# Left-over tokens of an expert in half blocks of 64 on 64-column tiles of TensorE

## The chip, the cores and the metric

One core of one Trainium2 chip. Times are device microseconds (us) of one execution. The kernel is timed in several executions and its median is given; each profile is one execution, and its "span" is some 2 us shorter than the time taken for the same run. Everything is float32.

## The reference, cut to what matters

Sliding-window attention over 8 x 576 = 4608 tokens of width 512 is followed by a mixture of eight experts, in which each token takes one expert (its own best, or that of the token before it).

```python
B, S, D, E, F = (8, 576, 512, 8, 1024)
...
            if s == 0 or local_gate[b, s] < 0.5:
                e = fresh_e
            else:
                e = prev_e if prev_e >= 0 else fresh_e
...
            h = np.maximum(x[b, s] @ w1[e], 0.0)
            out[b, s] = p[e] * (h @ w2[e])
```

## The kernel before

The expert part works in blocks of tokens that share an expert. Six early blocks of 128 tokens come from the first three sequences; then eight big blocks of 256; what is left of each expert is rounded up to small blocks of 128. Eighteen small blocks run always, which is just enough for these inputs; up to three more stand under a condition. Each block fetches its expert's weights (two loads of 2 MB by SyncE) and gathers its rows (an indirect DMA, issued by GpSimd). TensorE then does, in order: first layer of block i, transposes of block i+1, second layer of block i. The output goes out as an indirect scatter, also issued by GpSimd.

```python
    def hidden(self, st, quiet, step):               # first layer
        n = len(st["slots"]) * P                     # 128 or 256 tokens
        each = 512 // n
        for g in range(FK // each):                  # FK = 8 pieces of the 1024 hidden columns
            hp = self.ps_h.tile([P, each, n], F32, name="hp")
            for i in range(each):
                m = g * each + i
                for kk in range(DK):                 # DK = 4
                    nc.tensor.matmul(hp[:, i, :], lhsT=st["w1"][:, kk, m * P:(m + 1) * P], rhs=st["xt"][:, kk, :n],
                                     start=(kk == 0), stop=(kk == DK - 1))
            ...                                      # ReLU on ScalarE or VectorE
    def result(self, st, step):                      # second layer
        for i, s in enumerate(st["slots"]):
            yp = self.ps_y.tile([P, D], F32, name="yp")
            for m in range(FK):
                nc.tensor.matmul(yp, lhsT=st["h"][:, m, i * P:(i + 1) * P], rhs=st["w2"][:, m, :],
                                 start=(m == 0), stop=(m == FK - 1))
            ...
            nc.scalar.activation(y, yp, Act.Copy, scale=st["pw"][:, s:s + 1])
            nc.gpsimd.indirect_dma_start(out=self.out[:, :], out_offset=..., in_=y, ...)
    def run(self, ctx, rt):
        ...
        used = nc.values_load(self.tabs["ej"][0:1, NBLK:NBLK + 1], ...)
        with tc.If(used > SURE):                     # extra blocks, asleep with these inputs
            for n in order[total:]:
                ...
```

After this part a check of the attention's range ("flag") decides on a second condition, the careful path, which is asleep too.

## Time and profile before

| | before |
|---|---|
| median of the first 3 runs | 737.21 us (736.51 to 738.21) |
| profiled run: time, span | 733.09 us, 731.3 us |
| attention, to the first expert matmul | 144.3 us |
| experts, to the start of TensorE's last second-layer matmul | 578.3 us |
| tail, from there to the end of the span | 8.7 us |

The three parts are cut at starts of TensorE instructions in the timeline.

### The profile page before, as it was taken

What the parts mean: (1) busy time and instruction counts of PE and PEld (TensorE: products, weight loads), DVE (VectorE), ACT (ScalarE), POOL (GpSimd) and SP (SyncE); (2) the same over time, 40 slices, a digit from 0 to 9 for tenths busy, and PEclk for the clock granted to TensorE, in tenths of its full rate; (3) what the DMA queues carried; (4) which work ended last, traced back from release to release, by engine and by line L of the source; (5) the groups of instructions that cost most, each with busy time, mean ns of one, the idle gap of its engine ahead of it and who ended that gap; (6) DMA issues with size and microseconds to landing.
All of it is one profiled execution on the core that took longest, in us unless ns stands there. A gap on an engine that the chain in (4) does not pass through costs nothing. (4 is left out here: it accounts for less than half of the span.)

```text
span 731.3 us, 12607 instructions
## 1 busy us (share of the span) xinstructions
PE 689.0 (94%) x5476; PEld 500.9 (68%) x5476; DVE 186.4 (25%) x433; ACT 130.6 (18%) x186; POOL 115.4 (16%) x128
## 2 busy tenths in 40 slices
PE   4879788799999999999999999999999999999995
PEld 3667676677767765766756757677767776776673
DVE  5866898739400101101101011000100010001000
ACT  2755455311111010110110100011001100110010
POOL 4311323111131111111111020111111111100010
PEclk9999999999999999999999999999999999999999
DMA  8999999998899854564465455688989889888500
GB/s 310 389 399 391 390 364 393 408 343 314 290 368 428 345 200 158 172 232 172 141 226 195 143 196 219 215 315 316 332 321 318 327 315 346 288 319 306 201 17 30
DMA packets 37555, 203.84 MB, mean 279 GB/s; under 512 B 3661, under 2 KB 3677, under 8 KB 29296
## 3 DMA queue, kind: packets, MB, share of 16 engines
q1 hardware_dynamic: 28544, 173.45, 65.0%
q0 software_dynamic: 8944, 29.45, 10.2%
q8 instruction: 47, 0.77, 0.4%
q14 instruction: 20, 0.16, 0.1%
HBM read 184.01 MB, written 19.92 MB: 279 GB/s over the span
## 5 line engine op out<-in xcount | busy, mean ns | idle before, releaser
L928 PEld LDWEIGHTS hp<-xt,w 128*128 128x128 f32 x2048 | 272.6, 191 | 28.7 <-issue 14.3
L928 PE MATMUL hp<-xt,w 128*128 128x128 f32 (+1 forms) x2048 | 287.7, 301 | 1.4 <-ACT xt L916 1.4
L942 PE MATMUL yp<-w,h 128*128 128x512 f32 x640 | 280.4, 592 | 0.0
L942 PEld LDWEIGHTS yp<-w,h 128*128 128x128 f32 x640 | 118.9, 190 | 136.8 <-issue 134.9
L932 DVE TENSOR_SCALAR h<-hp 128x512 f32<-128x512 f32 x34 | 23.5, 691 | 473.5 <-issue 362.0
L947 ACT ACTIVATE y<-yp,pw 128x512 f32<-128x512 f32 x40 | 27.5, 687 | 358.5 <-PE yp L942 336.2
L948 POOL DMA_INDIRECT out_dram<-y,idx x40 | 41.1, 1027 | 302.7 <-ACT y L947 275.9
L886 POOL DMA_INDIRECT xg<-xs,idx x40 | 40.2, 1004 | 208.1 <-PE tp L915 190.0
L253 PE MATMUL sp<-w 64*64 64x128 f32 (+1 forms) x1296 | 47.4, 281 | 12.8 <-DMA w<-in_q_dram 7.0
L253 PEld LDWEIGHTS sp<-w 64*64 64x64 f32 x1296 | 40.7, 144 | 24.6 <-issue 10.5
L934 ACT ACTIVATE h<-hp 128x512 f32<-128x512 f32 x46 | 27.5, 597 | 159.2 <-PE hp L928 159.2
L282 PE MATMUL xo<-vb,p 128*64 128x74 f32 x576 | 46.2, 231 | 8.0 <-issue 3.8
L272 DVE TENSOR_TENSOR p<-p,mask 128x1024 f32<-128x1024 f32 x36 | 47.0, 1305 | 21.4 <-ACT p L269 21.0
L282 PEld LDWEIGHTS xo<-vb,p 128*64 128x64 f32 x576 | 40.2, 137 | 13.1 <-issue 6.0
L282 PE MATMUL xo<-va,p 128*64 128x74 f32 x576 | 46.0, 231 | 2.7 <-issue 2.1
L269 ACT ACTIVATE p<-sp 128x1024 f32<-128x1024 f32 x36 | 36.9, 1024 | 49.7 <-PE sp L253 45.1
L282 PEld LDWEIGHTS xo<-va,p 128*64 128x64 f32 x576 | 40.1, 137 | 2.4 <-issue 1.6
L291 DVE TENSOR_TENSOR x<-xo,allr 128x512 f32<-128x512 f32 x36 | 24.5, 680 | 2.5 <-DMA xs<-x 2.5
L229 POOL COPY vb<-va 64x1184 f32<-64x1184 f32 x9 | 10.9, 1216 | 87.5 <-PE xo L282 56.3
L915 PE MATMUL tp<-ident,xg 128*128 128x128 f32 x160 | 22.8, 273 | 0.0
L916 DVE COPY xt<-tp 128x512 f32<-128x512 f32 x32 | 21.2, 679 | 0.0
L915 PEld LDWEIGHTS tp<-ident,xg 128*128 128x128 f32 x160 | 18.7, 142 | 0.9
(203 smaller groups left out, 199.3 us busy)
## 6 DMA issues: line engine op xcount, KB each, us to landing
w<-in_w_dram SPq DMA_DIRECT2D x64, 2048.0 KB, 8.8
va<-in_v_dram SPq DMA_DIRECT2D x9, 1184.0 KB, 12.5
vtt<-in_vt_dram SPq DMA_DIRECT2D x9, 1024.0 KB, 10.2
xs<-x POOLq DMA_DIRECT2D x9, 1024.0 KB, 12.6
w<-in_k_dram SPq DMA_DIRECT2D x17, 512.0 KB, 11.6
w<-in_q_dram SPq DMA_DIRECT2D x17, 512.0 KB, 13.4
xg<-xs,idx POOLq DMA_INDIRECT x40, 8.2
out_dram<-y,idx POOLq DMA_INDIRECT x40, 8.2
```

The costliest lines, as they stand in the source:

```text
L253: nc.tensor.matmul(sp[c * WIN:(c + 1) * WIN, j, a:b], lhsT=kt[h, hp, block * WIN:(block + 1) * WIN], rhs=qt[h, hp, a:b], start=True, stop= ...
L269: nc.scalar.activation(p, sp, Act.Exp, scale=DH ** -0.5)
L272: nc.vector.tensor_tensor(p, p, m.to_broadcast([P, 2, SC]), op=Alu.mult)
L282: nc.tensor.matmul(xo[par * WIN:(par + 1) * WIN, j, s * VW:(s + 1) * VW], lhsT=p[:, j, b * WIN:(b + 1) * WIN], rhs=w[:, s, 2 * hp + j, :], ...
L291: nc.vector.tensor_tensor(x[:, :, hp].rearrange("p c j d -> p j c d"), o[:, :, :, :DH], rr.to_broadcast([P, 2, 4, DH]), op=Alu.mult)
L886: self.nc.gpsimd.indirect_dma_start(out=x, out_offset=None, in_=self.xs[:rows, :], in_offset=bass.IndirectOffsetOnAxis(ap=idx[:, s:s + 1], ...
L915: nc.tensor.transpose(tp[:, kk, :], x[:, kk * P:(kk + 1) * P], self.ident)
L928: nc.tensor.matmul(hp[:, i, :], lhsT=st["w1"][:, kk, m * P:(m + 1) * P], rhs=st["xt"][:, kk, :n], start=(kk == 0), stop=(kk == DK - 1))
L934: nc.scalar.activation(o, hp, Act.Relu)
L942: nc.tensor.matmul(yp, lhsT=st["h"][:, m, i * P:(i + 1) * P], rhs=st["w2"][:, m, :], start=(m == 0), stop=(m == FK - 1))
L947: nc.scalar.activation(y, yp, Act.Copy, scale=st["pw"][:, s:s + 1])
L948: nc.gpsimd.indirect_dma_start(out=self.out[:, :], out_offset=bass.IndirectOffsetOnAxis(ap=st["idx"][:, s:s + 1], axis=0), in_=y, in_offse ...
```

## The change

An expert's left-over of up to 64 tokens goes into a half block. Its matmuls would have only 64 rows of output, so they run in pairs on two column tiles of 64: in the first layer each takes half of a piece's hidden columns, in the second layer each takes half of the output columns. The result therefore lies as two half rows on two halves of the partitions, and is scattered as half rows. The router gets the counts and places for the half blocks, the order puts one half block after every second big block, and a zero row that the gathers use for empty places moves into a tile of another pool.

(Lines left out are marked `...`; remarks after `#` are not in the code.)

```diff
-NSM = (SMALL + E * (P - 1)) // P
-SURE = SMALL // P + E // 2
+HF = P // 2
+NSM = (SMALL + E * (HF - 1)) // P
+SURE = SMALL // P, E // 2          # 14 small blocks and 4 half blocks run always
...
-        self.shifted(ns, rest, P - 1, P.bit_length() - 1)
+        self.shifted(ns, rest, HF - 1, P.bit_length() - 1)
...
+        vec.scalar_tensor_tensor(limh, ns, float(P), lim, Alu.mult, Alu.add)
...
+        vec.tensor_tensor(nh, cnt, limh, op=Alu.is_gt)
...
             self.nc.gpsimd.indirect_dma_start(
-                out=x, out_offset=None, in_=self.xs[:rows, :],
-                in_offset=bass.IndirectOffsetOnAxis(ap=idx[:, s:s + 1], axis=0))
+                out=x[:n], out_offset=None, in_=self.xs[:rows, :],
+                in_offset=bass.IndirectOffsetOnAxis(ap=idx[:n, s:s + 1], axis=0))
...
-                    nc.tensor.matmul(hp[:, i, :], lhsT=st["w1"][:, kk, m * P:(m + 1) * P], rhs=st["xt"][:, kk, :n],
-                                     start=(kk == 0), stop=(kk == DK - 1))
+                    for f in range(0, P, st["rows"]):
+                        a = slice(f, f + st["rows"])
+                        nc.tensor.matmul(hp[a, i, :], lhsT=st["w1"][:, kk, m * P:(m + 1) * P][:, a],
+                                         rhs=st["xt"][:, kk, :n], start=(kk == 0), stop=(kk == DK - 1))
...
+            for m in range(FK):
+                for i in range(2):
+                    nc.tensor.matmul(yp[i * HF:(i + 1) * HF, :w], lhsT=st["h"][:, m, :HF],
+                                     rhs=st["w2"][:, m, i * w:(i + 1) * w], start=(m == 0), stop=(m == FK - 1))
...
+            nc.scalar.activation(y[:, :w], yp[:, :w], Act.Copy, scale=self.tabs["pwh"][:, s:s + 1])
+            nc.gpsimd.indirect_dma_start(
+                out=self.out.rearrange("n (i d) -> (n i) d", i=2),
+                out_offset=bass.IndirectOffsetOnAxis(ap=self.tabs["idxh"][:, s:s + 1], axis=0),
+                in_=y[:, :w], in_offset=None, bounds_check=2 * N - 1, oob_is_err=False)
...
-        with tc.If(used > SURE):
-            for n in order[total:]:
...
+        with tc.If(more > 0):       # up to 3 small and 4 half blocks
+            for n in [*range(NB + SURE[0], NB + NSM), *range(NB + NSM + SURE[1], NBLK)]:
```

More of the change, by code (lines that the diff above doesn't have):

```diff
@@ L47 @@
 SMALL = LEFT - NB * BIG
-NSM = (SMALL + E * (P - 1)) // P
-SURE = SMALL // P + E // 2
-NBLK = NB + NSM
-NS = SM0 + NSM
+HF = P // 2
+NSM = (SMALL + E * (HF - 1)) // P
+SURE = SMALL // P, E // 2
+NBLK = NB + NSM + E
+HF0 = SM0 + NSM
+NS = HF0 + E
 NEG = -1.0e9
@@ L88 @@
     tabs = dict(idx=const.tile([P, NS], U32, name="idx"), pw=const.tile([P, NS], F32, name="pw"),
-                ej=const.tile([1, NBLK + 1], I32, name="ej"), idx1=const.tile([P, FIRST], U32, name="idx1"),
+                ej=const.tile([1, NBLK + 1], I32, name="ej"), idxh=const.tile([P, E], U32, name="idxh"),
+                pwh=const.tile([P, E], F32, name="pwh"), idx1=const.tile([P, FIRST], U32, name="idx1"),
                 pw1=const.tile([P, FIRST], F32, name="pw1"), ej1=const.tile([1, FIRST], I32, name="ej1"))
@@ L96 @@
     nc.gpsimd.dma_start(out=wgs, in_=wg)
-    zrow = const.tile([1, D], F32, name="zrow")
-    nc.vector.memset(zrow, 0.0)
-    nc.gpsimd.dma_start(out=xs[N:N + 1, :], in_=zrow)
     ok = const.tile([P, 1], F32, name="ok")
@@ L107 @@
         ex = Experts(fast, tc, ring, *moe)
+        zrow = ex.xp.tile([P, D], F32, name="xg")[:1]
+        nc.vector.memset(zrow, 0.0)
+        nc.gpsimd.dma_start(out=xs[N:N + 1, :], in_=zrow)
         attention(tc, ring, q, k, v3, vt, xs, lt, ok, wg2s, ident, rt, ex)
@@ L773, in table @@
         vec.tensor_scalar(at, at, float(N), 0.0, Alu.add, Alu.max)
-        vec.tensor_scalar(idx, at, float(N), None, Alu.min)
+        vec.tensor_scalar(at, at, float(N), None, Alu.min)
+        vec.tensor_copy(idx, at)
         vec.tensor_tensor(pw, t[:, 2], t[:, 3], op=Alu.add)
         vec.tensor_tensor(pw, pw, t[:, 4], op=Alu.add)
+        return at
     def first(self, psum):
@@ L837, in second @@
         vec.tensor_tensor(soff, send, ns, op=Alu.subtract)
+        limh = tl("limh", P, E)
+        vec.scalar_tensor_tensor(limh, ns, float(P), lim, Alu.mult, Alu.add)
+        nh = tl("nh", P, E)
+        vec.tensor_tensor(nh, cnt, limh, op=Alu.is_gt)
+        hend = tl("hend", P, E)
+        vec.tensor_tensor_scan(hend, nh, self.zero[:, :E], 0.0, Alu.add, Alu.add)
+        hoff = tl("hoff", P, E)
+        vec.tensor_tensor(hoff, hend, nh, op=Alu.subtract)
         off = tl("off", P, E)
@@ L843, in second @@
         vec.scalar_tensor_tensor(step, step, float(SM0 * P), lim, Alu.add, Alu.subtract)
+        steph = tl("steph", P, E)
+        vec.tensor_tensor(steph, hoff, send, op=Alu.subtract)
+        vec.tensor_scalar(steph, steph, float(P), float((HF0 - SM0) * P), Alu.mult, Alu.add)
         CE = [P, CV, E]
@@ L849, in second @@
         vec.tensor_tensor(pl, pl, mid(off).to_broadcast(CE), op=Alu.add)
+        yield 6.0, False
+        plh = tl("plh", *CE)
+        vec.tensor_tensor(plh, self.rank, mid(limh).to_broadcast(CE), op=Alu.is_ge)
+        vec.tensor_tensor(plh, plh, mid(steph).to_broadcast(CE), op=Alu.mult)
+        vec.tensor_tensor(pl, pl, plh, op=Alu.add)
         vec.tensor_scalar(none, self.rank[:, :C1], 0.0, float(2 * N), Alu.is_lt, Alu.mult)
@@ L854, in second @@
         ej = tabs["ej"]
-        self.experts_of(ej[:, :NBLK], NBLK, [(NB, bend), (NSM, send)])
-        vec.tensor_copy(ej[:, NBLK:], send[0:1, E - 1:])
-        yield 10.0, False
-        yield from self.table(psum, slice(0, CV), NS, lo, hi, tabs["idx"], tabs["pw"])
+        self.experts_of(ej[:, :NBLK], NBLK, [(NB, bend), (NSM, send), (E, hend)])
+        more = tl("more", 1, 1)
+        vec.tensor_scalar(more, hend[0:1, E - 1:], float(SURE[1]), None, Alu.is_gt)
+        vec.scalar_tensor_tensor(ej[:, NBLK:], send[0:1, E - 1:], float(SURE[0]), more, Alu.is_gt, Alu.max)
+        yield 6.0, False
+        at = yield from self.table(psum, slice(0, CV), NS, lo, hi, tabs["idx"], tabs["pw"])
+        for i in range(2):
+            vec.tensor_scalar(tabs["idxh"][i * HF:(i + 1) * HF], at[:HF, HF0:], 2.0, float(i), Alu.mult, Alu.add)
+            vec.tensor_copy(tabs["pwh"][i * HF:(i + 1) * HF], tabs["pw"][:HF, HF0:])
 class Experts:
@@ L882, in rows @@
             slots = range(2 * n, 2 * n + 2) if n < NB else range(SM0 + n - NB, SM0 + n - NB + 1)
-        st.update(x=[], slots=slots, idx=idx, pw=pw)
+        st.update(x=[], slots=slots, idx=idx, pw=pw, rows=P)
+        if n >= NB + NSM:
+            st.update(half=n - NB - NSM, rows=HF)
         for s in slots:
             x = (self.xp if n < 0 else self.xq).tile([P, D], F32, name="xg")
+            n = st["rows"]
             self.nc.gpsimd.indirect_dma_start(
-                out=x, out_offset=None, in_=self.xs[:rows, :],
-                in_offset=bass.IndirectOffsetOnAxis(ap=idx[:, s:s + 1], axis=0))
+                out=x[:n], out_offset=None, in_=self.xs[:rows, :],
+                in_offset=bass.IndirectOffsetOnAxis(ap=idx[:n, s:s + 1], axis=0))
             st["x"].append(x)
@@ L909, in turn @@
     def turn(self, st, quiet):
-        nc = self.nc
+        nc, n = self.nc, st["rows"]
         st["xt"] = xt = self.wk.tile([P, DK, BIG], F32, name="xt")
@@ L914, in turn @@
             for kk in range(DK):
-                nc.tensor.transpose(tp[:, kk, :], x[:, kk * P:(kk + 1) * P], self.ident)
-            (nc.scalar.copy if quiet else nc.vector.tensor_copy)(xt[:, :, i * P:(i + 1) * P], tp)
+                nc.tensor.transpose(tp[:, kk, :n], x[:n, kk * P:(kk + 1) * P], self.ident[:n, :n])
+            (nc.scalar.copy if quiet else nc.vector.tensor_copy)(xt[:, :, i * P:i * P + n], tp[:, :, :n])
     def hidden(self, st, quiet, step):
         nc = self.nc
-        n = len(st["slots"]) * P
+        n = len(st["slots"]) * st["rows"]
         st["h"] = h = self.wk.tile([P, FK, BIG], F32, name="h")
@@ L927, in hidden @@
                 for kk in range(DK):
-                    nc.tensor.matmul(hp[:, i, :], lhsT=st["w1"][:, kk, m * P:(m + 1) * P], rhs=st["xt"][:, kk, :n],
-                                     start=(kk == 0), stop=(kk == DK - 1))
+                    for f in range(0, P, st["rows"]):
+                        a = slice(f, f + st["rows"])
+                        nc.tensor.matmul(hp[a, i, :], lhsT=st["w1"][:, kk, m * P:(m + 1) * P][:, a],
+                                         rhs=st["xt"][:, kk, :n], start=(kk == 0), stop=(kk == DK - 1))
             o = h[:, g * each:(g + 1) * each, :n]
-            if g % 2 and not quiet:
+            if (g % 2 or "half" in st) and not quiet:
                 nc.vector.tensor_relu(o, hp)
@@ L938, in result @@
         nc = self.nc
+        if "half" in st:
+            s, w = st["half"], D // 2
+            yp = self.ps_y.tile([P, D], F32, name="yp")
+            for m in range(FK):
+                for i in range(2):
+                    nc.tensor.matmul(yp[i * HF:(i + 1) * HF, :w], lhsT=st["h"][:, m, :HF],
+                                     rhs=st["w2"][:, m, i * w:(i + 1) * w], start=(m == 0), stop=(m == FK - 1))
+            y = self.wk.tile([P, D], F32, name="y")
+            nc.scalar.activation(y[:, :w], yp[:, :w], Act.Copy, scale=self.tabs["pwh"][:, s:s + 1])
[3 more added lines that the diff above has]
+                in_=y[:, :w], in_offset=None, bounds_check=2 * N - 1, oob_is_err=False)
+            step()
+            return
         for i, s in enumerate(st["slots"]):
@@ L965, in run @@
         side = rt.second(lambda: ps_r.tile([P, SC], F32, name="r"))
-        sure = NB + SURE
         pause = 0.0
@@ L981, in step @@
                     late.append(self.fetch(0, spare=True))
-        order = [-1 - n for n in range(FIRST)] + list(range(NBLK))
-        total = FIRST + sure
+        order = [-1 - n for n in range(FIRST)]
+        halves = list(range(NB + NSM, NB + NSM + SURE[1]))
+        for n in range(NB):
+            order.append(n)
+            if n % 2 and halves:
+                order.append(halves.pop(0))
+        order += halves + list(range(NB, NB + SURE[0]))
+        total = len(order)
         self.turn(jobs[0], True)
@@ L990, in run @@
             if n:
-                jobs.append(self.fetch(n, spare=n > 0 and n % 3 == 0))
+                jobs.append(self.fetch(n, spare=n > 0 and (i + 2 - FIRST) % 3 == 0))
             self.hidden(jobs[i], quiet, step)
@@ L999, in run @@
             self.result(jobs[i], step)
-        used = nc.values_load(self.tabs["ej"][0:1, NBLK:NBLK + 1], min_val=0, max_val=NSM,
-                              skip_runtime_bounds_check_because="a count of blocks, at most NSM")
-        with tc.If(used > SURE):
-            for n in order[total:]:
+        more = nc.values_load(self.tabs["ej"][0:1, NBLK:NBLK + 1], min_val=0, max_val=1,
+                              skip_runtime_bounds_check_because="the larger of two comparisons")
+        with tc.If(more > 0):
+            for n in [*range(NB + SURE[0], NB + NSM), *range(NB + NSM + SURE[1], NBLK)]:
                 st = self.fetch(n, spare=n % 3 == 0)
```

## The prediction

> **What bounds the kernel now.** I read the page first: engine shares, then the forty slices. TensorE's matmuls cover 94% of the span, the next engine 25%.
>
> ```profile
> PE 689.0 (94%) x5476; PEld 500.9 (68%) x5476; DVE 186.4 (25%) x433; ACT 130.6 (18%) x186; POOL 115.4 (16%) x128
> ...
> PE   4879788799999999999999999999999999999995
> ...
> PEclk9999999999999999999999999999999999999999
> DMA  8999999998899854564465455688989889888500
> ```
>
> The reader is to see that TensorE is at nine tenths from the ninth slice to the one before the last, at full clock, while the transfers have room in every slice of the second half. The page's chain that ended last has only the tail in it (the flag and the last scatter), so it says nothing of the stages. Busy matmuls alone don't prove a bound either, so I cut the span into stages at the block boundaries that the timeline of TensorE shows: attention to 144 us, six early blocks of 128 tokens to 229, eight big blocks of 256 tokens to 461, eighteen small blocks of 128 tokens to 723, and the tail.
>
> ```profile
> core 0: us, PE busy (x) PEld busy (x) DVE busy (x) ACT busy (x) POOL busy (x), PEclk, DMA share, GB/s
> ...
> 229.00:461.00 232.00, 232.00 (x846) 154.74 (x845) 20.01 (x31) 21.98 (x35) 32.76 (x33) 1.00 0.56 206
> 461.00:723.00 262.00, 262.00 (x1514) 191.56 (x1512) 22.57 (x35) 23.11 (x36) 28.83 (x29) 1.00 0.76 274
> 723.00:731.30 8.30, 0.45 (x2) 0.08 (x1) 0.42 (x2) 0.69 (x1) 0.98 (x1) 0.84 0.11 34
> ```
>
> From 229 to 723 us TensorE has no idle time at all. DMA engines are busy 56% of the big stage and 76% of the small one. The timeline of one small block shows what a block is made of:
>
> ```profile
> 607.85 7.31 PE L928 MATMUL hp<-xt,w 128*128 128x128 f32 x64
> 615.00 0.60 PE L915 MATMUL tp<-ident,xg 128*128 128x128 f32 x4
> 615.43 7.03 PE L942 MATMUL yp<-w,h 128*128 128x512 f32 x16
> 622.30 3.96 PE L928 MATMUL hp<-xt,w 128*128 128x128 f32 x34
> ```
>
> Columns: start, length, engine, line, operation, tiles, form, count. A float32 matmul of the source is two instructions here (32 in the source, 64 in the row). From start to start: 7.15 us for the 64 of the first layer (111.7 ns each), 0.43 for the four transposes of the next block, 6.87 for the 16 of the second layer (429 ns each), together **14.45 us a small block**, whatever the number of tokens in it. The same view at a big block gives 28.43 us, with 64 first-layer matmuls of 256 columns in 13.81 us, so 215.8 ns each. Check of the whole: 24 x 14.45 + 8 x 28.43 = 574 us of the 579 between 144 and 723; the rest is the router's own matmuls. So the stage is a sum of TensorE times, and what a block loses there the end loses.
>
> [...]The attention part already uses 128x64 column tiles in pairs, float32, 128 rows, so the trace of before can be asked:
>
> ```profile
> 83.35 0.23 PE L282 MATMUL xo<-vb,p 128*64 128x74 f32 x1
> 83.39 0.23 PE L282 MATMUL xo<-va,p 128*64 128x74 f32 x1
> 83.42 0.23 PE L282 MATMUL xo<-vb,p 128*64 128x74 f32 x1
> 83.45 0.23 PE L282 MATMUL xo<-va,p 128*64 128x74 f32 x1
> ```
>
> Two such matmuls, with their own weight loads, start every 64.5 ns[...]. [...]from the last of these to the first of a 64x64 mode is 155 ns in nearly all 24 cases, some 0.1 us more than the next of its kind would have taken.[...]
>
> **The change part by part.** From the inputs I worked out the routing: after the six early and eight big blocks the experts' left-overs are 9, 115, 105, 165, 177, 222, 274 and 725 tokens. Before: rounded up to 128 they are 18 small blocks, exactly the 18 that run unconditionally. After: 14 small blocks and four half blocks (left-overs of 9, 37, 49 and 18), again exactly the number that runs unconditionally, so the conditional extra blocks stay asleep. Four small blocks become four half blocks; the number of weight fetches (4.2 MB each) stays.
>
> A half block on TensorE:
> - Transposes: four, still 128 weight columns each: 4 x 109 ns = 0.43 us.
> - First layer: 128 instructions as 64 pairs of 64 columns.[...]
> - Second layer: 16 pairs of 256 columns at 215.8 ns: 3.45 us instead of 6.87.
> - Mode switches: its transposes (64 rows) lie between full-array matmuls of the block before, and the next block's transposes between its two layers; six changes at 0.1 us: 0.6 us.
> - A new wait: [...]one ReLU follows the last matmul instead of one per half. In the trace of before the ReLU begins 0.35 us after the last first-layer matmul's start and takes 0.69; the transposes that hide it are 0.43 us before a small block (one case) and 0.87 before a big one (three). I estimate 0.55 us once and 0.15 three times: 0.25 on average.
>
> Sum 0.43 + 3.75 + 3.45 + 0.6 + 0.25 = 8.5 us, so 5.95 us less than 14.45. **Four blocks: 23.8 us.**
>
> The router gets some ten tiny VectorE operations (0.17 us each), three over 296 elements (0.48 each) and tables 41 wide instead of 37: about 5 us of VectorE, which is idle for 42.6 us in the before trace between the finished index at 201 us and its next ReLU. The index may come 3 to 8 us later; its first user, the transposes of the first big block at 229 us, is 28 us away and the gather takes 8. Its 37 table matmuls grow by about 8 ns each: +0.3 us on TensorE. Scatter as half rows: 128 pieces of 1 KB instead of rows of 2 KB, four times, off the path. Zero row, tail: unchanged.
>
> 737.2 - 23.8 + 0.3 = **713.7 us**.
>
> **The rivals.** (a) Weights become the bound: a half block needs the same 4.2 MB in 8.5 us. Against: they are placed one after every second big block. The big stage moved 206 GB/s x 232 us = 47.8 MB; with four more fetches and gathers, 65.6 MB in 266 us is 247 GB/s, under the 274 that the small stage carries with no TensorE idle. The fetch of a block starts when the one three places before it is done, and a half block has two of the 28 us blocks ahead of it. If wrong: some microseconds back per half block, 718 to 728. (b) The pairs don't pair at 64 columns: 256 instructions in 3.75 us is one per 15 ns. In attention the densest 5 us hold 158 matmuls with as many loads, 16 ns an instruction, so it is near what has been seen, not beyond doubt. If the first layer gains nothing, each half block costs 11.9 us: 727. (c) The router's tail delays the first big block: 20 us of slack speak against it; if it did, +5 us.[...]
>
> **Range and chances.** All rivals but none of size push up; down, there is the switch term, which may be half (-1.2 us), and the wait (-1). So 710.5 to 718.5 holds it 8 times in 10. The 2% line is at 722.5; only (a) or (b) in full cross it: faster 0.93, same 0.06, slower 0.01.
>
> **What would show it.** In the changed trace: half-block first layers of about 3.75 us and second layers of about 3.45 on 128x64 tiles; gaps of about 0.1 us at their edges; TensorE without DMA waits before any first layer; 14 small blocks still at 14.45 us and big ones at 28.43; six early blocks ending within 1 us of where they did. The prediction is wrong if pairs start every 112 ns rather than 58, if a first layer waits for a w tile, or if the conditional blocks run.

The sum for a half block came to 8.5 us, and for the four to 23.8. The working of its largest term, 3.75 us for the first layer, used figures that no trace shows; the 3.75 us, or 58 ns a pair, are the author's estimate. Rival (d) is cut for a mechanism that it named: mode changes of 0.3 us instead of 0.1, +5 us, the upper end of the range. The traces of before carry the argument almost as far: single matmuls of 128, 256 and 512 columns start every 109 (transposes), 215.8 and 429 ns there, and on a straight line through these lie, as an estimate, 64 ns for 74 columns and 56 for 64. So the attention's pairs, one every 64.5 ns, take about as long as one matmul alone would, and 64 pairs of 64 columns 3.6 us, which makes the half block 8.3 us.

## The result, and the profile after

The changed kernel takes 728.67 us (median of 4 runs, 727.22 to 731.18) against 737.03 us for the kernel before (4 runs). The ratio is 0.9888, with a 95% interval of 0.9857 to 0.9919: an improvement of 1.1%, clear of noise but under the 2% line that the prediction draws, where 3.2% had been predicted. A ratio here is the mean time of one kernel's fast runs over that of the other's of the same rounds, so it is not quite the ratio of the medians.

The page of the changed kernel, in the lines that answer to those of before:

```profile
PE 670.0 (92%) x5796; PEld 487.4 (67%) x5796; DVE 187.2 (26%) x450; ACT 127.0 (18%) x182; POOL 116.7 (16%) x128
...
PE   4888888899999999999999999999999999999980
...
PEclk9999999999999999999999999999999999999995
DMA  8999999998879955674394557647988989787000
```

Look at the right end. TensorE is idle in the last slice (18 us) and the clock there is halved; before, the last slice was half busy. The stages of the changed kernel, cut at the same instructions (columns as in the prediction's table of stages):

```profile
core 0: us, PE busy (x) PEld busy (x) DVE busy (x) ACT busy (x) POOL busy (x), PEclk, DMA share, GB/s
...
147.39:703.20 555.81, 555.51 (x3211) 394.45 (x3211) 77.87 (x180) 54.85 (x89) 78.91 (x77) 1.00 0.70 267
703.20:725.30 22.10, 0.84 (x3) 0.08 (x1) 0.42 (x2) 0.69 (x1) 0.98 (x1) 0.58 0.05 13
```

The expert part shrank from 578.3 to 555.8 us, 22.5 us less, still without idle time on TensorE. But 22 us pass after it in which no engine computes for more than 1 us and DMA moves next to nothing; before it was 8.7 us. **TensorE finished 19 us earlier and the program ended 6 us earlier.** The mean clock of 0.976 (before 0.994) is not a cause: it is full (1.00) in the expert part, and low in the long tail where TensorE has no work (0.58) and in short stretches of attention (0.94 over the whole of it).

Here is the half block that the prediction was about, in the timeline of TensorE (start, length, engine, line, operation, tiles, form, count):

```profile
268.21 13.98 PE L962 MATMUL hp<-xt,w 128*128 128x256 f32 x64
282.12 0.46 PE L947 MATMUL tp<-ident,xg 64*128 64x64 f32 x4
282.51 14.00 PE L992 MATMUL yp<-w,h 128*128 128x512 f32 x32
296.44 4.18 PE L962 MATMUL hp<-xt,w 128*64 128x64 f32 x128
300.55 1.09 PE L947 MATMUL tp<-ident,xg 128*128 128x128 f32 x8
301.57 3.67 PE L979 MATMUL yp<-w,h 128*64 128x256 f32 x32
305.18 14.08 PE L962 MATMUL hp<-xt,w 128*128 128x256 f32 x64
```

From one big block's first layer to the next, with a half block between, are 36.97 us; a big block alone takes 28.43. That is 8.54 us for the half block. The first layer that follows it starts 0.10 us slower than others do (28.53 us to the block after, in the trace), so it costs 8.64 us in all, and 8.5 had been predicted. So the change does what it was meant to do, and the miss lies elsewhere.

What fills the tail? The views by engine leave out a sequencer's own instructions, but the view of a source line lists them (minimum/median/maximum in ns, first and last start). In the changed kernel, the condition for extra blocks (L1057), the one for the careful path (L116) and the program's end (L1100), those of GpSimd:

```profile
L1057 POOLq EVENT_SEMAPHORE  x4: 17/42/3590, 705.4 to 709.1; - x4
...
L1057 POOLq INC_SWDGE_SEM  x1: 2031/2031/2031, 709.2 to 709.2; - x1
...
L116 POOLq INC_SWDGE_SEM  x1: 1996/1996/1996, 714.8 to 714.8; - x1
...
L1100 POOLq DRAIN  x3: 46/103/7587, 716.8 to 724.9; - x3
```

And the same three places of the kernel before:

```profile
L1002 POOLq EVENT_SEMAPHORE  x3: 17/43/43, 724.8 to 724.9; - x3
...
L1002 POOLq INC_SWDGE_SEM  x1: 387/387/387, 725.0 to 725.0; - x1
...
L114 POOLq INC_SWDGE_SEM  x1: 336/336/336, 729.3 to 729.3; - x1
...
L1045 POOLq DRAIN  x3: 46/103/809, 729.7 to 731.0; - x3
```

Three instructions of GpSimd that have nothing to do with the half blocks take 2.0, 2.0 and 7.6 us instead of 0.4, 0.3 and 0.8: 10.1 us more. In addition GpSimd waits 3.6 us for the last scatter at the first condition, just after its branch (705.2 us in the same view); the kernel before got past this place while that scatter was under way. Together that is about the 13.3 us by which the tail grew. It had to be found out why.

### The profile page after: what moved, and what is told of

The parts are those of the page before. It is cut to its first block, busy times and chain, and to the rows that moved or that the text cites. A ratio compares the mean times of both kernels' runs of the same rounds, so it can differ in the third digit from the quotient of the medians.

```text
span 725.2 us, 13252 instructions
## 1 busy us (share of the span) xinstructions
PE 670.0 (92%) x5796; PEld 487.4 (67%) x5796; DVE 187.2 (26%) x450; ACT 127.0 (18%) x182; POOL 116.7 (16%) x128
## 3 DMA queue, kind: packets, MB, share of 16 engines
q0 software_dynamic: 8688, 28.93, 10.1%
## 5 line engine op out<-in xcount | busy, mean ns | idle before, releaser
L962 PEld LDWEIGHTS hp<-xt,w 128*128 128x128 f32 (+1 forms) x2304 | 258.7, 179 | 29.8 <-issue 14.6
L962 PE MATMUL hp<-xt,w 128*128 128x128 f32 (+2 forms) x2304 | 275.7, 287 | 1.7 <-ACT xt L948 1.7
L992 PE MATMUL yp<-w,h 128*128 128x512 f32 x576 | 252.7, 593 | 0.0
L992 PEld LDWEIGHTS yp<-w,h 128*128 128x128 f32 x576 | 107.1, 190 | 123.7 <-issue 122.4
L966 DVE TENSOR_SCALAR h<-hp 128x512 f32<-128x512 f32 x34 | 23.5, 691 | 447.1 <-issue 306.0
L998 POOL DMA_INDIRECT out_dram<-y,idx x36 | 37.3, 1037 | 277.2 <-ACT y L997 249.9
L997 ACT ACTIVATE y<-yp,pw 128x512 f32<-128x512 f32 x36 | 24.7, 687 | 315.2 <-PE yp L992 294.2
L918 POOL DMA_INDIRECT xg<-xs,idx x40 | 40.8, 1019 | 194.7 <-PE tp L947 157.0
L274 DVE TENSOR_TENSOR p<-p,mask 128x1024 f32<-128x1024 f32 x36 | 44.5, 1235 | 24.6 <-ACT p L271 24.5
L284 PEld LDWEIGHTS xo<-vb,p 128*64 128x64 f32 x576 | 41.9, 141 | 12.4 <-issue 6.9
L271 ACT ACTIVATE p<-sp 128x1024 f32<-128x1024 f32 x36 | 36.9, 1024 | 54.0 <-PE sp L255 46.4
L947 PE MATMUL tp<-ident,xg 128*128 128x128 f32 (+1 forms) x160 | 22.5, 271 | 0.0
L948 DVE COPY xt<-tp 128x512 f32<-128x512 f32 (+1 forms) x32 | 20.1, 647 | 0.0
L947 PEld LDWEIGHTS tp<-ident,xg 128*128 128x128 f32 (+1 forms) x160 | 17.8, 141 | 2.1 <-issue 1.3
```

Of the source, the lines that this page charges most:

```text
L271: nc.scalar.activation(p, sp, Act.Exp, scale=DH ** -0.5)
L274: nc.vector.tensor_tensor(p, p, m.to_broadcast([P, 2, SC]), op=Alu.mult)
L284: nc.tensor.matmul(xo[par * WIN:(par + 1) * WIN, j, s * VW:(s + 1) * VW], lhsT=p[:, j, b * WIN:(b + 1) * WIN], rhs=w[:, s, 2 * hp + j, :], ...
L918: self.nc.gpsimd.indirect_dma_start(out=x[:n], out_offset=None, in_=self.xs[:rows, :], in_offset=bass.IndirectOffsetOnAxis(ap=idx[:n, s:s ...
L947: nc.tensor.transpose(tp[:, kk, :n], x[:n, kk * P:(kk + 1) * P], self.ident[:n, :n])
L962: nc.tensor.matmul(hp[a, i, :], lhsT=st["w1"][:, kk, m * P:(m + 1) * P][:, a], rhs=st["xt"][:, kk, :n], start=(kk == 0), stop=(kk == DK - 1))
```

## The experiments

Sixteen kernels ran; all gave right results. Seven of them were timed in several executions. The other nine (`b_g64`, `b_g128`, `b_zrow`, `a_one64`, `a_two64`, `b_g64x4`, `b_spq`, `a_dbl64`, `b_x18`) ran once, under the profiler, and their state is unknown; so they are read by the lengths of their parts and instructions alone. Those repeat: the drain took 809 ns in both profiles of the kernel before and 7587 ns in both of the changed one. The theories named in the expectations: L, the long tail is chance of an execution; K, it belongs to the kernel; H, the scatter as half rows causes it; X, the larger conditional part; G, gathers of 64 rows; R, the sum of what GpSimd has issued by the end. (Where `a_g128`'s expects the long tail of R, R did not yet go by the number of rows.) For each run the three parts of the span are given, and the two small instructions (SWDGE-semaphore increments) and the drain of GpSimd.

### Controls

`c_before` and `c_after` are the two kernels unchanged.

> The kernel before, unchanged, as a control. In the first profiles TensorE's last matmul started at 722.6 us (before) and 703.3 (after), 19 us apart, but the spans were only 6 us apart: the tail after TensorE was 8 us before and 21 after, and attention ended 3 us later. Theory L (luck of one execution): the tail varies between executions of the same kernel; this copy would then show tails other than 8 us, up to 20. Theory K (it belongs to the new kernel): this copy has its 8 us tail again, span 731 to 735, ratio 1.00.

> The changed kernel, unchanged, as a control. Theory L: the tail may be short this time, near 8 us, and the span near 712. Theory K: tail again 20 us or more, span 724 to 730, ratio 0.988 again. The 3 us in attention: if it is of the execution and not of the kernel, first early-block matmul between 144 and 147.5 us at random in both kernels.

| | attention | experts | tail | small, small, drain | median, ratio |
|---|---|---|---|---|---|
| first profile, before | 144.3 | 578.3 | 8.7 | 0.39, 0.34, 0.81 | 737.03 |
| first profile, after | 147.4 | 555.8 | 22.0 | 2.03, 2.00, 7.59 | 728.67, 0.989 |
| `c_before` | 150.2 | 578.3 | 8.6 | 0.39, 0.34, 0.81 | 736.59, 0.998 |
| `c_after` | 148.5 | 556.2 | 22.2 | 2.03, 2.00, 7.59 | 729.44, 0.989 |

K holds and L falls: tail and experts repeat within 0.4 us. Attention, on the other hand, lies anywhere from 144.3 to 153.0 us over all profiles, in kernels of both kinds and with the same code; those few microseconds are of the execution, and probably they are what makes medians scatter by 2 us and more. From here on the reading is by parts.

### Half-row scatter (`e_fullrow`) and conditional blocks (`e_noextra`)

```diff
-            nc.scalar.activation(y[:, :w], yp[:, :w], Act.Copy, scale=self.tabs["pwh"][:, s:s + 1])
+            for i in range(2):
+                a = slice(i * HF, (i + 1) * HF)
+                nc.scalar.activation(y[:HF, i * w:(i + 1) * w], yp[a, :w], Act.Copy, scale=self.tabs["pwh"][a, s:s + 1])
             nc.gpsimd.indirect_dma_start(
-                out=self.out.rearrange("n (i d) -> (n i) d", i=2), ... idxh ..., in_=y[:, :w]
+                out=self.out[:, :], ... ap=self.tabs["idx"][:HF, HF0 + s:HF0 + s + 1] ..., in_=y[:HF]
```

> The changed kernel, but each half block's output is put together as 64 whole rows by two evictions and scattered as rows of 2 KB through the same view of the output as everywhere else. Theory H (the half-row scatters, or their second view of the output, make the tail): tail back to about 8 us, time about 716. Theory L or X (extra conditional blocks): tail as in the changed kernel, time within 2 us of it (the second small eviction lies off TensorE's path).

Measured: tail 22.0 us, 2.03, 2.00 and 7.59; 729.5 us, ratio 0.989. H falls. The half-row scatter and the second view of the output cost nothing, and scattering whole rows gains nothing either.

`e_noextra` leaves out the condition with the extra blocks (`with tc.If(more > 0): ...`).

> The changed kernel without the conditional extra blocks, which do not run with these inputs (result still right). Theory X (the waits on entry to and exit from that conditional part are what is long): the tail loses one of its two long stretches, 4 to 6 us shorter or more. Theory H: most of the tail stays, about 16 us or more. Theory L: anything.

Measured: tail 17.0 us, 724.4 us, ratio 0.982. The condition's own wait (3.6 us) and one of the two small instructions are gone; the other (2.04) and the drain (7.58) are as slow as before. So X explains over a third of the extra tail (5.0 of 13.3 us, 1.6 of them the slowness of the small instruction that went), and not why the instructions are slow.

### Gathers of 64 rows (`a_g128`, `b_g64`, `b_g128`, `b_zrow`)

What both scatter variants had in common was that the half blocks gather 64 rows. `a_g128` gathers 128 for them, the upper 64 of which nobody reads:

```diff
-                out=x[:n], ... ap=idx[:n, s:s + 1]
+                out=x, ... ap=idx[:, s:s + 1]
```

> The controls showed that the long tail belongs to the changed kernel: there two small instructions and the last drain of GpSimd take 2.0, 2.0 and 7.6 us in every execution, 0.4, 0.3 and 0.8 in the kernel before. This run is the changed kernel with the half blocks' rows gathered as 128 rows (the index holds a harmless row for the upper 64), the only indirect transfers that had 64 channels in it. Theory G (a transfer of 64 channels leaves GpSimd slow at the end): drain about 0.8 us, tail about 9 us, time about 717. Theory R[...]: tail as in the changed kernel, 22 us, time 729.

Measured: experts 555.8, tail 12.4 us; **717.85 us, ratio 0.974** (0.969 to 0.979). One line of index shape brings back 10 us. The small instructions take 0.37 and 0.34 us again, and the drain:

```profile
L1099 POOLq DRAIN  x3: 46/103/809, 713.0 to 714.4; - x3
```

The other three put suspects into the kernel before: a needless gather of 64 rows, or of 128, ahead of the first small block's gather; and the changed kernel's zero row.

```diff
+            for m in (P // 2, P) if n == NB else (P,):      # b_g64;  (P, P) in b_g128
                 self.nc.gpsimd.indirect_dma_start(out=x[:m], ... ap=idx[:m, s:s + 1] ...)
```

> The kernel before plus one needless gather of 64 rows ahead of the gather of 128 of the first small block. Theory G: the drain becomes 7.6 us and the tail of 8.6 us grows to about 18 or 22. Theory R: either.

> Control for the run with 64 rows: the needless gather has 128 rows. Theory G: tail of 8.6 us stays, drain 0.8 us. Theory R[...]: tail may change.

> The kernel before with the changed kernel's zero row (in a tile that the gathers use later) in place of its own. Theory G: tail stays at 8.6 us. If the row's move is what matters, drain 7.6 us and tail about 20 us.

Measured: tails of 8.9, 8.8 and 8.6 us; drains of 0.89, 0.89 and 0.81 us. A gather of 64 rows does not by itself make GpSimd slow, so G in its plain form falls although `a_g128` had seemed to prove it. The zero row is innocent. A small trace is left: one transfer more, of either size, makes the drain 0.08 us longer. (The experts took 579.7 us with the gather of 128 rows and 578.3 with that of 64; the 1.4 us were not followed up.)

### How many (`a_one64`, `a_two64`, `b_g64x4`), and the condition again (`a_g128_noextra`)

In the changed kernel only the first, or the first two, half blocks keep 64 rows (`n = HF if st.get("half") == 0 else P`, and `in (0, 1)`); in the kernel before each of the first four small blocks gets a needless gather of 64 rows.

> The changed kernel with only the first half block's gather left at 64 rows, all others at 128. With four the drain took 7.6 us, with none 0.8. If each gather of 64 rows adds its share: drain about 2.5 us, the two small instructions about 0.8 us. If one is enough: 7.6 and 2.0. If it takes several: 0.8 and 0.4, as the kernel before with one needless gather of 64 rows had it.

> The same with the first two half blocks at 64 rows. If each adds its share: drain about 4.2 us. If one is enough: 7.6. If it takes more than two: 0.8.

> The kernel before with a needless gather of 64 rows in each of the first four small blocks. If the number of gathers of 64 rows decides, whatever the kernel: drain 7.6 us and a tail about 10 us longer than 8.6. If it needs the changed kernel (what its half blocks do otherwise): drain 0.8 to 1.1 us.

Measured drains: 0.81, 0.73 and 0.97 us; tails 12.4, 11.9 and 8.8 us. Neither "each adds its share" nor "one is enough", and four in the kernel before do next to nothing (0.16 us). What sorts these runs is the number of rows (pieces of one partition each; a half row counts as one) that GpSimd's transfers carry in all, against the kernel before: 64 fewer, 128 fewer and 256 more here; 256 fewer in the changed kernel and 512 fewer in `e_fullrow`, the two with the long drain.

`a_g128_noextra` is `a_g128` without the condition.

> The changed kernel with gathers of 128 rows and without the conditional extra blocks. The tail with 128-row gathers was still 12.4 us against 8.6: GpSimd waits 3.9 us for the last scatter ahead of the condition. If that wait comes from the condition alone: tail 7 to 9 us, time 713 to 715, ratio about 0.968. If it is something else: tail 12 us, time 717.9.

Measured: tail 8.9 us, span 711.5 us; median 716.28 us (713.26 to 720.21), ratio 0.974. The tail did what was expected. The median was 1 us above the range; of the four executions (713.26, 719.02, 713.54, 720.21) only the first was profiled, so that attention's scatter made the others longer is likely and not shown. The remaining 3.5 us of tail are the condition's. The view of its line shows the wait of 3590 ns in the changed kernel and 43 in the one before. Seven extra blocks make fourteen GpSimd transfers, and by the trace these transfers take turns on eight semaphores (102 to 109 in the kernels before and after), so one of the fourteen needs the semaphore of the last scatter; three extra blocks made six, which the last scatter's was not among. That the condition is the cause is shown. The reading by semaphores was argued from the trace, but a run made for another purpose bears it out: `b_x18`, below, gives the three extra blocks of the kernel before nine transfers instead of six, and there too GpSimd stands still at the condition, for 4.1 us (729.9 to 734.0), until the last scatter has landed.

### The sum of rows and transfers (`b_spq`, `a_dbl64`, `b_x18`)

Three tests of R from three sides. `b_spq` takes 256 rows away from GpSimd in the kernel before, by issuing two small, unrelated loads elsewhere. `a_dbl64` is the changed kernel with every half block's gather of 64 rows done twice: eight such gathers, but as many rows as before. `b_x18` gives the kernel before a second gather of 128 rows in all 18 small blocks.

```diff
-    nc.gpsimd.dma_start(out=wg2s, in_=wg2)          # b_spq
+    nc.sync.dma_start(out=wg2s, in_=wg2)
-    nc.gpsimd.dma_start(out=wgs, in_=wg)
+    nc.sync.dma_start(out=wgs, in_=wg)
```

```diff
+            for _ in range(2 if "half" in st else 1):       # a_dbl64
                 self.nc.gpsimd.indirect_dma_start(out=x[:n], ...)
```

```diff
+            for m in (P, P) if n >= NB else (P,):           # b_x18
                 self.nc.gpsimd.indirect_dma_start(out=x[:m], ...)
```

> The kernel before with its two small loads of gate weights issued by SyncE instead of GpSimd, nothing else. [...]Theory R[...]: [...]the kernel before gets the slow end: 2.0, 2.0 and 7.6 us, tail some 17 us, span near 743 to 746. Theory G (gathers of 64 rows in the half blocks' company): tail 8.6 us as ever.

> The changed kernel with each half block's gather of 64 rows issued twice: eight gathers of 64 rows[...]. Theory R: fast end, 0.4, 0.3 and 0.8 us, tail 12 us. Theory G: slow end, 2.0, 2.0 and 7.6 us, tail 22 us.

> The kernel before with a needless second gather of 128 rows in all eighteen small blocks. Theory R: the drain grows by about 0.08 us for each (0.81 to 0.89 with one): about 2.2 us, the two small instructions about 0.8 us. If the slow end is a mere switch: drain 0.9 us.

`b_spq`, the kernel before with not one half block in it:

```profile
L1002 POOLq INC_SWDGE_SEM  x1: 2002/2002/2002, 733.7 to 733.7; - x1
...
L114 POOLq INC_SWDGE_SEM  x1: 1961/1961/1961, 739.8 to 739.8; - x1
...
L1045 POOLq DRAIN  x3: 40/107/7425, 741.8 to 749.8; - x3
```

Its tail is 18.8 us instead of 8.6: **the same slow end, made by taking two small loads off GpSimd.** (Its span of 750 us is above the expected 746 because attention took 153.0 us in this execution; the experts took their 578.3.) `a_dbl64`: 0.37, 0.34 and 0.81 us, tail 12.0 us, fast as R has it, with twice the gathers of 64 rows. `b_x18`:

```profile
L1046 POOLq DRAIN  x3: 46/103/2279, 739.3 to 742.1; - x3
```

2.28 us, where 2.2 was expected: not a switch, but a time that grows. (The small instructions took 0.73 and 0.70 us; its tail is 14.7 us, because of the wait at the condition told above.) All in one table. Its last two columns were worked out after the runs and are explained below it:

| run | rows, against before | transfers, against before | drain, us | pieces an engine | late transfer, from the end |
|---|---|---|---|---|---|
| `e_fullrow` | -512 | 0 | 7.59 | 1005 | none |
| `b_spq` | -256 | -2 | 7.42 | 1019 | none |
| after, `c_after`, `e_noextra` | -256 | 0 | 7.58 to 7.59 | 1021 | none |
| `a_two64` | -128 | 0 | 0.73 | 1029 | last |
| `a_one64` | -64 | 0 | 0.81 | 1033 | 2nd |
| before, `c_before`, `b_zrow`, `a_g128`, `a_g128_noextra`, `a_best` | 0 | 0 | 0.81 | 1037 | 2nd |
| `a_dbl64` | 0 | +4 | 0.81 | 1041 | 2nd |
| `b_g64` / `b_g128` | +64 / +128 | +1 | 0.89 | 1042 / 1046 | 3rd |
| `b_g64x4` | +256 | +4 | 0.97 | 1057 | 4th |
| `b_x18` | +2304 | +18 | 2.28 | 1199 | 20th |

Bytes do not sort these runs: `b_spq` moves 0.08 MB less than the kernel before and has a long drain, `a_two64` 0.26 MB less and a short one. Nor do the packets that the page counts in GpSimd's queue: 8880 both in `b_spq`, with a long drain, and in `a_dbl64`, with a short one.

Two regularities stand out. The long drain comes between 128 and 256 rows below the kernel before: 0.73 us in `a_two64`, 7.42 in `b_spq` and 7.59 in the changed kernel. And the drain goes in steps of 0.082 us, but not by the transfers added: four more cost two steps in `b_g64x4` and none in `a_dbl64`. Theory R fits as far as it is a matter of counting: the kernel before (1037 in the table's fifth column) passes a certain count shortly before its end, and the changed kernel (1021) just misses it and has the long drain, at the end, where nothing hides it.

The kept traces have a sign of the point where the count is passed. Each of the last scatters starts 0.28 us after ScalarE's output is ready, but in every run without the long drain one starts 1.2 us later than that, and in no run with it does any. Here are two in a row of the kernel before in the timeline of GpSimd (in brackets its idle time before them and what ended it), and then the one of the changed kernel in the place of the second:

```profile
695.76 0.98 POOL L948 DMA_INDIRECT out_dram<-y,idx  x1 [13.47 <-ACT y L947]
711.42 0.99 POOL L948 DMA_INDIRECT out_dram<-y,idx  x1 [14.67 <-issue]
```

```profile
690.81 0.98 POOL L998 DMA_INDIRECT out_dram<-y,idx  x1 [13.47 <-ACT y L997]
```

The last column of the table says which transfer is the late one. (In `b_x18` it lies among the gathers and is told by the gap after the transfer in front of it, 1.73 us instead of 0.31.) The drain follows from it: 0.65 us plus 0.082 for each transfer from the late one to the end, in all five cases from one to twenty. And its place follows from a count made up for the purpose: a transfer's pieces divided over the 16 DMA engines, and one more for its packets of 4 bytes (1472 in the trace of the kernel before, 16 for each of the 92 transfers). The late transfer is in every run the first that brings this count above 1023, and where the count ends below, none is late. 1023 is fitted to these runs, and no run tested it in advance; `a_dbl64` and `b_g64`, in which a transfer ends at a count of just 1023 and just 1024, allow no other whole number.

The counts, the late transfer and the times are shown, and the drains of the three runs above came as counting rows and transfers had them. What happens in the hardware at the late transfer and in the drain is not shown. Nor does the count account for everything. As an estimate, (7.59 - 0.73) / 0.082 is 84 transfers more than the one of `a_two64`, so a long drain is as long as that of 85 transfers, and the program has 92.

### Both causes of the tail removed (`a_best`)

`a_best` is `a_g128` with the two conditions made one: inputs that need extra blocks now take the careful path, which has them. The extra blocks thus stay possible, at a higher price for such inputs, which was not timed.

```diff
-        ex.run(fast, rt)
+        ex.run(fast, rt, False)                     # no condition for extra blocks here
...
     flag(tc, ok, bad, ident)
+    nc.vector.tensor_tensor(bad, bad, tabs["ej"][:, NBLK:], op=Alu.max)
```

> The changed kernel with gathers of 128 rows for the half blocks, and with the condition for extra blocks joined to the one for the careful path (inputs that need extra blocks then take the careful path, which has them), so that no condition stands between the last scatter and the end. Theory: drain 0.8 us, GpSimd's 3.9 us wait ahead of a condition gone, tail 8.5 to 9.5 us, expert part 556 us, time 712 to 717, ratio about 0.97.

Measured: experts 555.8, tail 8.4 us, 0.37 and 0.81 us (one small instruction and the drain); **716.74 us (712.14 to 719.25, 6 runs), ratio 0.972** (0.968 to 0.976). This beats both kernels. Against `a_g128` (0.974) the intervals overlap, but the tail is 4.0 us shorter. It reaches the predicted range.

## Why the prediction was wrong

**The bound, right.** TensorE's sum of block times sets the end of the expert part: 22.1 to 22.5 us came out of it, and 23.5 (23.8 less 0.3 for the router) had been predicted. No first layer waited for weights; the TensorE share of the expert part is 555.51 of 555.81 us.

**The half block, right in its sum, with terms that were off both ways.** By the starts of the single instructions in the trace, pairs of 64 columns start every 58.4 ns, with one gap of 0.19 us in the middle that nobody expected: the first layer takes 3.97 us, not the 3.75 of the forecast's sum. Pairs of 256 columns start every 216 ns (215.8), so the second layer takes the 3.46 us expected. The transposes take 0.25 us rather than 0.43, since those of 64 rows start 62 ns apart and not the 109 of those of 128. The six mode changes cost more than the 0.6 us estimated, about 0.97: each makes the interval across it 91 to 100 ns longer, and the first interval after it another 48 to 104 ns, which the prediction had left out. The new wait for the single ReLU showed only before the small block, 0.37 us (0.55), and not before the big ones (0.15). One half block is 8.64 us in three cases and 9.03 in the one with the wait, a mean of 8.74 against 8.5. That the sum came so near is in part luck: the mode changes were set too low and the transposes too high.

**The router, right.** From the first expert matmul to the first big block it took 92.40 us instead of 92.08: +0.32 us, as predicted, and its 37 table matmuls start every 91 ns instead of 83. Its longer tables delayed nothing.

**The rivals.** (a) weights, (b) pairs that don't pair and (c) the router's delay stayed away, as argued. (d), costlier mode changes, came in part: 0.16 us a change, against 0.1 estimated and 0.3 feared. One reading was loose, though nothing rests on it: the transfers do not have room in every slice of the second half; three of its slices stand at 9.

**The failed step** is four words: "Zero row, tail: unchanged." The tail was taken over from the profile of before as a constant of 8.7 us, and it became 22.0. Of the 13.3 us, 10.1 are GpSimd's closing work, which depended on the number of rows and transfers that it had issued over the whole program (shown by `a_g128`, `b_spq`, `a_dbl64`, `b_x18`), and the other 3.2 (3.5 when the condition is taken out) are the wait at the condition, which the larger conditional part had moved behind the last scatter (shown by `a_g128_noextra` and `a_best`). Sum of the two misses: 13.3 us of tail and about 1 us of TensorE, against 15 us between 713.7 predicted and 728.7 measured; the rest is within attention's scatter. With the tail repaired the kernel stands at 716.7 us.

The prediction did look at GpSimd's transfers, but only at whether each lay beside TensorE's work. It asked what each costs when it is issued, and not what is owed for it when the program ends.

**Open:** what GpSimd does in the drain and in the 1.2 us before the late transfer, and why a long drain is that of 85 transfers and not of 92; no record of the trace shows it. The 1023 pieces an engine are a fit to these runs that has yet to predict one.

## What to carry to other kernels

When a change takes time off the engine that bounds a kernel, check the tail as a part of its own: cut the span at the bounding engine's last instruction in both profiles, and list the sequencers' own instructions there. The kernels of this study issue 90 to 110 transfers from GpSimd and ended in a drain of 7.4 to 7.6 us or of 0.73 to 2.28, and 128 rows fewer or more were enough to go from one to the other; padding four gathers from 64 to 128 rows was worth 10 us (`a_g128`). And dead code under a condition was not free: GpSimd waited 3.6 us for the last scatter where the changed kernel passed it over.
